# Seven block products for eight in the second MLP's first product, on one Trainium2 core

## The chip, the cores and the metric

The kernel runs on one core of one Trainium2 chip. The metric is device time of one execution in microseconds (us). The names of the engines are PE (TensorE, matrix products; PEld are its weight loads), DVE (VectorE), ACT (ScalarE), POOL (GpSimd) and SP (SyncE, which here issues every DMA).

## The reference

Attention through 32 packed queries, then two MLPs in a row over 4608 tokens of width 512. The attention output becomes `x` with shape 4608 x 512, and then:

```python
# first MLP:  w_a, w_b 512 x 1536, w_out 1536 x 512
x = ((x @ w_a) * (x @ w_b)) @ w_out
# second MLP: w_in 512 x 2048, w_out 2048 x 512
h = x @ w_in
g = h * np.clip(h + 3.0, 0.0, 6.0) / 6.0
out = g @ w_out
```

## The kernel before, in words

The program is one stream per engine, in an order written out by hand (`tc.manual_schedule`, L513): each engine takes its instructions in the order in which the Python code issues them, and waits by semaphore for what an instruction reads or overwrites. Work is set beside other work by calling small functions ("units") at chosen places of a loop.

Products in near-float32 accuracy are made of three matmuls of a rounded type (`mm3`, L57): an operand x is split into a high part, a copy in that type made by ACT, and a low part, x minus its high part, made by POOL or DVE; then hi x hi, hi x lo and lo x hi are added up in PSUM.

The first stage (L601 to L658) runs attention and the first MLP, in 4 groups of 2 batches x 12 steps (one step: 128 columns of F1). It also converts the weights of both MLPs from float64 words, piece by piece (`f64_load`, `f64_round`, `piece_units`), into float32 copies in DRAM; those of the second MLP go to `p2f`. These conversion tiles lie in the pool `main`. The pool `att` is closed at the first step of the last group (L607), and `p2a` takes its place; there the first token tile and the first weights of the second MLP are loaded and split ahead, as background units spread over the steps of that last group (L609 to L614). The first MLP's result goes to DRAM as `y1d`, transposed: 4 blocks of 128 channels x 4608 tokens.

The second MLP (L662 to L721) takes 9 tiles of 512 tokens. Per tile, for each of 16 blocks m of 128 hidden channels: `h_unit` makes h (4 channel blocks x 3 matmuls of 512 columns) into one of four PSUM banks, ACT makes `relu(h/6 + 0.5)`, DVE `min(.,1) * h`, ACT the high part and DVE the low part. Two blocks behind, `o_unit` adds the block's share to the output: 4 row blocks x 3 matmuls of 512 columns, in four PSUM banks that collect over all 16 m. All weights of the second MLP stay in SBUF, split once (`p2_weights`): three blocks ahead, the others during the first tile. The next tile's tokens are loaded and split from m = 10 on (`y_part`).

Of the kernel before, what the change touches and what calls it, by code (L numbers as in the profile page):

```python
# [8 lines left out]
F32 = mybir.dt.float32  # L9
# [13 lines left out]
P = 128  # L23
# [6 lines left out]
T2 = 512  # L30
# [14 lines left out]
def tile_kernel(ctx: ExitStack, tc: tile.TileContext, qT, kT, vn, pT, wab, wo1, win, wo2, out):  # L45
# [11 lines left out]
    def mm3(ps, l_hi, l_lo, r_hi, r_lo, first, last):  # L57
        pe.matmul(ps, lhsT=l_hi, rhs=r_hi, start=first, stop=False)  # L58
        pe.matmul(ps, lhsT=l_hi, rhs=r_lo, start=False, stop=False)  # L59
        pe.matmul(ps, lhsT=l_lo, rhs=r_hi, start=False, stop=last)  # L60
# [42 lines left out]
    y1d = dram.tile([DM // P, P, NT], F32, name="y1d")  # L103

# [247 lines left out]

    def piece_units():
# [3 lines left out]
        if m >= NM1:  # L357
            o = main.tile([P, CP], F32, tag="p2f", name=f"p2f{m}_{i}", bufs=3)
# [14 lines left out]
        u = f64_round(main, raw64.pop(k), o, f"p{m}_{i}")  # L373
# [96 lines left out]
    win_t, wo2_t = {}, {}  # L470

    def p2_weights(pool_, m, which):

        r = pool_.tile([P, CP], F32, tag="r2", name=f"r2_{m}{which}", bufs=3)
        sp.dma_start(r, p2f[m, which])

        def split():
            if which == 0:
                hi = pool_.tile([P, 4, P], F32R, tag=f"win_hi{m}", name=f"win_hi{m}")
                lo = pool_.tile([P, 4, P], F32R, tag=f"win_lo{m}", name=f"win_lo{m}")  # L480
                win_t[m] = (hi, lo)
                x = r.rearrange("p (k n) -> p k n", k=4)
            else:
                hi = pool_.tile([P, DM], F32R, tag=f"wo2_hi{m}", name=f"wo2_hi{m}")
                lo = pool_.tile([P, DM], F32R, tag=f"wo2_lo{m}", name=f"wo2_lo{m}")
                wo2_t[m] = (hi, lo)
                x = r
            act.copy(hi, x)
            pool.tensor_sub(lo, x, f32(hi))

        return split

    y_t = {}

    def y_part(pool_, tt, kk):

        r = pool_.tile([P, T2], F32, tag="r2", name=f"yr{tt}_{kk}", bufs=3)
        sp.dma_start(r, y1d[kk, :, tt * T2:(tt + 1) * T2])

        def split():  # L500
            if kk == 0:
                y_t[tt] = (
                    pool_.tile([P, 4, T2], F32R, tag="y_hi", name=f"y_hi{tt}"),
                    pool_.tile([P, 4, T2], F32R, tag="y_lo", name=f"y_lo{tt}"),
                )
# [76 lines left out]
    p2_list = [(m, w) for m in range(NM2) for w in range(2)]  # L582
    PRE = 3
# [17 lines left out]
    for t in range(NSTEP):  # L601
# [27 lines left out]
        if t == NG * NM1 - NM1:  # L629
            sp.dma_start(*stores[-1])  # L630
# [31 lines left out]
    with (  # L662
# [3 lines left out]
        gq = {}  # L666

        def h_unit(tt, m):
            ps = ps2.tile([P, T2], F32, tag="h", name=f"h{tt}_{m}", bufs=4)
            yh, yl = y_t[tt]  # L670
            wh, wl = win_t[m]
            for kk in range(4):
                mm3(ps, wh[:, kk, :], wl[:, kk, :], yh[:, kk, :], yl[:, kk, :], kk == 0, kk == 3)
            r = p2b.tile([P, T2], F32, tag="r", name=f"r{tt}_{m}", bufs=2)
            act.activation(r, ps, AF.Relu, bias=half_b, scale=1.0 / 6.0)  # L675
            u = p2b.tile([P, T2], F32, tag="u", name=f"u{tt}_{m}", bufs=2)
            dve.scalar_tensor_tensor(u, in0=r, scalar=1.0, in1=ps, op0=ALU.min, op1=ALU.mult)  # L677
            hi = p2b.tile([P, T2], F32R, tag="g2_hi", name=f"g2_hi{tt}_{m}", bufs=4)
            lo = p2b.tile([P, T2], F32R, tag="g2_lo", name=f"g2_lo{tt}_{m}", bufs=4)
            act.copy(hi, u)  # L680
            dve.tensor_sub(lo, u, f32(hi))
            gq[tt, m] = (hi, lo)
# [3 lines left out]
        def o_unit(tt, m):  # L686
            hi, lo = gq.pop((tt, m))
            wh, wl = wo2_t[m]
            for j in range(T2 // P):
                if m == 0:  # L690
                    y2[j] = ps2.tile([P, DM], F32, tag=f"o{j}", name=f"o{tt}_{j}", bufs=1)
                ts = slice(j * P, (j + 1) * P)
                mm3(y2[j], hi[:, ts], lo[:, ts], wh, wl, m == 0, m == NM2 - 1)
                if m == NM2 - 1:
                    o = p2b.tile([P, DM], F32, tag="o", name=f"os{tt}_{j}", bufs=4)
# [66 lines left out]
```

## Time and profile before

| | before |
|---|---|
| median of 3 runs | 1605.7 us (1605.18 to 1605.84) |
| profiled execution, its own time | 1605.02 us |
| its span, first to last instruction | 1603.0 us |
| PE busy / PEld | 1538.5 us (96%) / 1327.5 us (83%) |
| DVE / ACT / POOL busy | 699.2 us (44%) / 621.0 us (39%) / 406.6 us (25%) |
| mean granted TensorE clock | 0.982 |
| DMA | 149.05 MB, mean 93 GB/s |

Busy times are sums over the whole span, and the stages differ: a share says little until it is read for one stage. Matmuls are pipelined, so that the time shown for one matmul is longer than the step from its start to the start of the next; where matmuls follow each other without a break, the step is what one of them costs. The granted clock is a share of full speed.

### The profile page before, as it was taken

Reading aid. Unit: us, or ns where it says so; the run is one execution under the profiler, and the core shown is the slowest. Engines: PE = TensorE matmul, PEld = TensorE weight load, DVE = VectorE, ACT = ScalarE, POOL = GpSimd, SP = SyncE. Lnnn points to the kernel's source line nnn. Section 1 sums busy time; section 2 is a strip of 40 time slices with the busy share of each in tenths; the row PEclk is TensorE's granted clock in tenths of the full one; section 3 lists DMA queues with packets and bytes.
Section 4 is the critical chain, followed back from the end, with each engine's and each line's share of the span. In section 5 each row is a group of like instructions: output and inputs, shape, how many; then the busy total and the mean of one; then the engine's idle time right before and its main releaser. Section 6 shows DMA issues by size and latency. Waiting matters only on the chain.

```text
span 1603.0 us, 26633 instructions
## 1 busy us (share of the span) xinstructions
PE 1538.5 (96%) x10840; PEld 1327.5 (83%) x10840; DVE 699.2 (44%) x1235; ACT 621.0 (39%) x1287; POOL 406.6 (25%) x426
## 2 busy tenths in 40 slices
PE   4598999989999899999999999999999999999999
PEld 2487999888988899999988888888888888888887
DVE  5677885555754666333333233232323232322322
ACT  4465644554555444443244222232222222222322
POOL 2566554353534445334344000000000000000000
PEclk8698999999999999999999999999999999999999
DMA  8665464645365432421143101000010101010000
GB/s 279 208 213 168 156 210 155 195 165 164 127 197 180 142 112 94 138 69 53 40 131 92 47 7 47 7 27 21 7 46 8 46 7 46 7 47 7 27 1 27
DMA packets 69754, 149.05 MB, mean 93 GB/s; under 512 B 7168, under 2 KB 25600, under 8 KB 69632
## 3 DMA queue, kind: packets, MB, share of 16 engines
q1 hardware_dynamic: 69632, 147.35, 28.0%
q8 instruction: 85, 1.39, 0.4%
q14 instruction: 37, 0.30, 0.1%
HBM read 110.62 MB, written 36.70 MB: 92 GB/s over the span
## 4 chain that ended last, share of the span: by engine, by line
PE 90%; DVE 4%; ACT 3%; issue 1%; DMA 1%; POOL 0%; SPq 0%; DVEq 0%; ACTq 0%
PE h L58 8%; PE o L58 8%; PE h L60 8%; PE o L60 8%; PE h L59 8%; PE o L59 8%; PE y L58 7%; PE y L59 6%; PE y L60 6%; PE ab L58 6%; PE ab L60 6%; PE ab L59 6%; PE pw L410 2%; PE s L174 1%; DVE cv_ap L87 1%
## 5 line engine op out<-in xcount | busy, mean ns | idle before, releaser
L677 DVE SCALAR_TENSOR_TENSOR u<-r,h 128x512 f32<-128x512 f32 x144 | 99.2, 689 | 454.1 <-ACT r L675 454.0
L675 ACT ACTIVATE r<-h,half_b 128x512 f32<-128x512 f32 x144 | 99.1, 688 | 441.1 <-PE h L60 441.1
L58 PE MATMUL ab<-at_hi,pw_hi 128*128 128x288 f32 x768 | 234.5, 305 | 21.5 <-ACT a L436 18.5
L60 PE MATMUL ab<-at_hi,pw_lo 128*128 128x288 f32 x768 | 229.8, 299 | 4.0 <-DVE pw_lo L416 4.0
L58 PE MATMUL y<-g_hi,wo_hi 128*128 128x288 f32 x768 | 232.7, 303 | 0.4 <-DVE acc L465 0.4
L59 PE MATMUL ab<-at_lo,pw_hi 128*128 128x288 f32 x768 | 229.5, 299 | 1.7 <-POOL at_lo L290 1.7
L59 PE MATMUL y<-g_lo,wo_hi 128*128 128x288 f32 x768 | 228.1, 297 | 0.0
L60 PE MATMUL y<-g_hi,wo_lo 128*128 128x288 f32 x768 | 227.4, 296 | 0.0
L58 PE MATMUL h<-y_hi,win_hi 128*128 128x512 f32 x576 | 226.2, 393 | 0.0
L58 PE MATMUL o<-wo_hi,g_hi 128*128 128x512 f32 x576 | 226.0, 392 | 0.0
L60 PE MATMUL h<-y_hi,win_lo 128*128 128x512 f32 x576 | 225.4, 391 | 0.0
L60 PE MATMUL o<-wo_hi,g_lo 128*128 128x512 f32 x576 | 225.2, 391 | 0.0
L59 PE MATMUL h<-y_lo,win_hi 128*128 128x512 f32 x576 | 225.0, 391 | 0.0
L59 PE MATMUL o<-wo_lo,g_hi 128*128 128x512 f32 x576 | 224.7, 390 | 0.0
L445 POOL TENSOR_TENSOR g_lo<-g,g_hi 128x288 fp32r<-128x288 f32 x192 | 162.0, 847 | 186.3 <-ACT g_hi L444 179.0
L438 DVE TENSOR_TENSOR g<-a,ab 128x288 f32<-128x288 f32 x192 | 86.8, 452 | 205.1 <-PE ab L60 142.9
L58 PEld LDWEIGHTS ab<-at_hi,pw_hi 128*128 128x128 f32 x768 | 147.1, 192 | 34.1 <-ACT a L436 20.8
L58 PEld LDWEIGHTS y<-g_hi,wo_hi 128*128 128x128 f32 x768 | 145.6, 190 | 19.1 <-issue 7.1
L60 PEld LDWEIGHTS ab<-at_hi,pw_lo 128*128 128x128 f32 x768 | 147.1, 191 | 4.5 <-DVE pw_lo L416 4.4
L59 PEld LDWEIGHTS ab<-at_lo,pw_hi 128*128 128x128 f32 x768 | 147.3, 192 | 2.2 <-POOL at_lo L290 2.2
L59 PEld LDWEIGHTS y<-g_lo,wo_hi 128*128 128x128 f32 x768 | 145.7, 190 | 0.0
L60 PEld LDWEIGHTS y<-g_hi,wo_lo 128*128 128x128 f32 x768 | 145.6, 190 | 0.0
(80 smaller groups left out, 2194.3 us busy)
## 6 DMA issues: line engine op xcount, KB each, us to landing
rab<-wabf SPq DMA_DIRECT2D x36, 512.0 KB, 4.4
f64p<-in_wo SPq DMA_DIRECT2D x28, 512.0 KB, 3.7
f64p<-in_wab SPq DMA_DIRECT2D x24, 512.0 KB, 4.4
k<-in_kT SPq DMA_DIRECT2D x16, 576.0 KB, 5.6
q<-in_qT SPq DMA_DIRECT2D x16, 576.0 KB, 5.0
ro<-wo1f SPq DMA_DIRECT2D x36, 256.0 KB, 2.9
y1d<-acc SPq DMA_DIRECT2D x64, 144.0 KB, 1.8
yr<-y1d SPq DMA_DIRECT2D x36, 256.0 KB, 3.5
```

Of the source, the lines that this page charges most:

```text
L58: pe.matmul(ps, lhsT=l_hi, rhs=r_hi, start=first, stop=False)
L59: pe.matmul(ps, lhsT=l_hi, rhs=r_lo, start=False, stop=False)
L60: pe.matmul(ps, lhsT=l_lo, rhs=r_hi, start=False, stop=last)
L87: dve.scalar_tensor_tensor(a, in0=w, scalar=0xC0000000, in1=a, op0=ALU.bitwise_and, op1=ALU.bitwise_or)
L174: pe.matmul(ps[c][o, :SH], lhsT=lhsT[r, q, :], rhs=kq_t[n, b, q // 2][r, q % 2, ts], start=True, stop=True)
L410: pe.matmul(ps[c][o, b, :], lhsT=l[r, b, q, :], rhs=w[r, q, :], start=True, stop=True)
L438: dve.tensor_mul(g32, a, ps[1])
L445: pool.tensor_sub(gl, g32, f32(gh))
L675: act.activation(r, ps, AF.Relu, bias=half_b, scale=1.0 / 6.0)
L677: dve.scalar_tensor_tensor(u, in0=r, scalar=1.0, in1=ps, op0=ALU.min, op1=ALU.mult)
```

## The change

Only the second MLP changes, and where its operands are prepared. Tokens now come in 6 tiles of 768 (two halves of 384), hidden channels in 8 pairs p of two 128-channel blocks. With the four 256-channel x 128-channel blocks of the weights of a pair as A (A21 and A22 are the second block's) and the four 256-channel x 384-token blocks of a token tile as B, the four blocks of h come from seven products:

- S1 = A21 + A22, S2 = S1 - A11, S3 = A11 - A21, S4 = A12 - S2 (weights); T1 = B12 - B11, T2 = B22 - T1, T3 = B22 - B12, T4 = B21 - T2 (tokens)
- M1 = A11 B11, M2 = A12 B21, M3 = S4 B22, M4 = A22 T4, M5 = S1 T1, M6 = S2 T2, M7 = S3 T3
- h(0,0) = M1 + M2; with U2 = M1 + M6 and U3 = U2 + M7: h(1,1) = U3 + M5, h(1,0) = U3 + M4, h(0,1) = U2 + M5 + M3

M2, M7, M4 and M3 are added in PSUM onto M1, M6, M6 + M7 and M5; the other sums are made by DVE from a copy of M1 (`s1`, by ACT) and PSUM. The products use two PSUM banks in turn, the output six (six row blocks of 128 tokens). Each product is 2 x 3 matmuls of 384 columns; the output product keeps its 3 matmuls of 512 columns per row block and hidden block. The output units of a pair run inside the next pair's pass: `before.pop()()` does the last split of the pair before and puts its 12 output units on a list, from which `o_units(n)` takes n; `some(n)` takes n of the waiting side units (weights, tokens).

The weight operands of a pair (7 blocks, high and low, 14 KB per partition) are built by `w_prep` from `p2f`: pair 0 during the last group of the first MLP, pair p + 1 during pass p of the first token tile; the float32 words go into a tile `raw` of one buffer, which the token tiles use too. Each is stored to a DRAM tensor `w2d`, and in the five later token tiles it is loaded from there, one pass ahead, into the other of two buffers (`p2a`, `p2b`). The output weights stay in SBUF. `y_units` loads a token tile, makes T1 to T4 on POOL and splits the seven operands; in the last pass of a tile each is replaced as soon as its product is done (`swap`).

Elsewhere: the conversion tiles (`f64_load`, `f64_round`, `p2f`) lie in `att`, and the last `p2f` store is issued ahead of closing `att`, not after that step's units are set up.

```diff
-T2 = 512
+TP, TH = 768, 384
+NW = NM2 // 2
...
+    w2d = dram.tile([NW, P, 14 * 256], F32, name="w2d")
...
-            raw64[k] = f64_load(main, src, f"p{m}_{i}")
+            raw64[k] = f64_load(att, src, f"p{m}_{i}")
...
+    PROD = {1: (0, "B11"), 2: (1, "B21"), 3: (6, "B22"), 4: (2, "T4"), 5: (3, "T1"), 6: (4, "T2"), 7: (5, "T3")}
...
+    def w_load(pool_, p, tt):
+        sp.dma_start(f32(w_tile(pool_, p, tt).rearrange("p h a k n -> p (h a k n)")), w2d[p])
+
+    def w_prep(rpool, pool_, p):
...
+        def load():
+            z["r"] = rpool.tile([P, 6, CP], F32, tag="raw", name=f"raw_w{p}")
+            for i in range(2):
+                sp.dma_start(z["r"][:, i], p2f[2 * p + i, 0])
+
+        def sums(lo):
...
+                if lo:
+                    pool.tensor_sub(s3, a11, a21)
+                    pool.tensor_sub(s4, a12, s2)
+                else:
+                    pool.tensor_add(s1, a21, a22)
+                    pool.tensor_sub(s2, s1, a11)
...
+        def parts(of, a, n):
...
+                act.copy(hi, x)
+                pool.tensor_sub(lo, x, f32(hi))
...
+        def wo_load():
+            for i in range(2):
+                sp.dma_start(z["r"][:, 4 + i], p2f[2 * p + i, 1])
...
+        return [load, wo_load, sums(0), sums(1), parts(0, 0, 2), parts(3, 2, 1), parts(4, 3, 4), store], lambda o: [wo_parts(o, 0), wo_parts(o, 1)]
+
+    def y_units(pool_, tt):
...
+        def load():
+            z["r"] = pool_.tile([P, 4, TP], F32, tag="raw", name=f"raw_y{tt}")
...
         if m == 0 and g + 1 == NG:
+            sp.dma_start(*stores[-1])
             es_att.close()
...
+            y_load, y_first, y_part = y_units(p2a, 0)
+            prep, wo_prep = w_prep(p2a, p2a, 0)
+            bg = [y_load, lambda: None, lambda: None] + y_first + [y_part[k] for k in (1, 6, 2, 7, 5, 4, 3)] + prep
...
+        def prod(ps, k, first):
+            a, n = PROD[k]
+            w = w_t[now[1]]
+            yh, yl = y_t[n]
+            for c in range(2):
+                mm3(ps, w[:, 0, a, c], w[:, 1, a, c], yh[:, c], yl[:, c], first and c == 0, c == 1, not first)
...
+        side.extend(wo_prep(p2b))
         for tt in range(NTT):
+            for p in range(NW):
...
+                if tt == 0 and p + 1 < NW:
+                    prep, wo_prep = w_prep(p2a, wpool, p + 1)
+                    side.extend(prep + wo_prep(p2b))
+                elif p + 1 < NW or more:
+                    side.append(lambda x=(wpool, nxt, tt + (p + 1) // NW): w_load(*x))
+                last = p == NW - 1 and more
+                if more and p == NW - 2:
+                    y_load, y_first, y_part = y_units(p2a, tt + 1)
+                    side.extend([y_load, lambda: None, lambda: None] + y_first)
...
+                x = bank2("x")
+                prod(x, 1, True)
+                s1 = tmp("s1", 2)
+                act.copy(s1, x)
+                if before:
+                    before.pop()()
+                swap(1)
+                o_units(2)
+                some(3)
+                y = bank2("y")
+                prod(y, 6, True)
+                u2 = plus("u2", 2, s1, y)
+                swap(6)
+                prod(x, 2, False)
+                gate(0, 0, x)
+                swap(2)
+                o_units(2)
+                some(2)
+                prod(y, 7, False)
+                u3 = plus("u3", 2, s1, y)
+                parts(0, 0)
+                swap(7)
+                x = bank2("z")
+                prod(x, 5, True)
+                c22 = plus("c22", 2, u3, x)
+                gate(1, 1, c22)
+                swap(5)
+                o_units(2)
+                some(2)
+                prod(y, 4, False)
+                c21 = plus("c21", 1, s1, y)
+                parts(1, 1)
+                gate(1, 0, c21)
+                swap(4)
+                prod(x, 3, False)
+                c12 = plus("c12", 2, u2, x)
+                parts(1, 0)
+                gate(0, 1, c12)
+                swap(3)
+                o_units(2)
+                some(2)
+                o_units(4)
+                some(9)
```

## Rows read from the trace of the kernel before

**Rows 1.** The page, parts 1 and 4: busy time by engine; the last chain.
```profile
PE 1538.5 (96%) x10840; PEld 1327.5 (83%) x10840; DVE 699.2 (44%) x1235; ACT 621.0 (39%) x1287; POOL 406.6 (25%) x426
...
PE 90%; DVE 4%; ACT 3%; issue 1%; DMA 1%; POOL 0%; SPq 0%; DVEq 0%; ACTq 0%
```

**Rows 2.** Busy by stretch: PE, PEld, DVE, ACT, POOL; clock, DMA share, GB/s.
```profile
600.00:800.00 200.00, 199.62 (x1802) 190.32 (x1801) 81.61 (x166) 82.12 (x200) 82.01 (x98) 1.00 0.24 78
...
1100.00:1200.00 100.00, 100.00 (x440) 82.38 (x440) 28.49 (x42) 26.63 (x42) 0.00 (x0) 1.00 0.07 22
```

**Rows 3.** Waits: total us, times, longest.
```profile
ACT r L675 <- PE h L60: 441.1, 140, 3.7
```

**Rows 4.** Timeline where the second MLP begins: start, duration, engine, operation [idle before].
```profile
799.85 0.29 PE L60 MATMUL y<-g_hi,wo_lo 128*128 128x288 f32 x1
...
807.45 0.29 PE L60 MATMUL y<-g_hi,wo_lo 128*128 128x288 f32 x1
807.58 0.40 PE L58 MATMUL h<-y_hi,win_hi 128*128 128x512 f32 x1
...
807.78 0.46 DVE L465 TENSOR_TENSOR acc<-y,acc 128x288 f32<-128x288 f32 x1 [0.74 <-PE y L60]
```

**Rows 5.** Timeline, the last matmul.
```profile
1599.01 0.39 PE L60 MATMUL o<-wo_hi,g_lo 128*128 128x512 f32 x1
```

**Rows 6.** Groups of instructions by form: busy us, mean ns, idle before.
```profile
L681 DVE TENSOR_TENSOR g_lo<-u,g_hi 128x512 fp32r<-128x512 f32 x144 | 99.8, 693 | 98.9 <-ACT g_hi L680 98.9
...
L465 DVE TENSOR_TENSOR acc<-y,acc 128x288 f32<-128x288 f32 x192 | 86.8, 453 | 95.8 <-PE y L60 95.1
...
L394 POOL TENSOR_TENSOR wo_lo<-ro,wo_hi 128x256 fp32r<-128x256 f32 x96 | 75.0, 781 | 139.4 <-ACT wo_hi L393 136.1 <-PE y L60 3.3
...
L393 ACT CAST wo_hi<-ro 128x256 fp32r<-128x256 f32 x96 | 39.6, 413 | 34.4 <-PE y L59 26.5 <-POOL ro L95 7.9
...
L489 POOL TENSOR_TENSOR wo_lo<-r,wo_hi 128x512 fp32r<-128x512 f32 x16 | 20.7, 1295 | 28.1 <-ACT wo_hi L488 16.2 <-PE o L60 11.9
...
L488 ACT CAST win_hi<-r 128x512 fp32r<-128x512 f32 x16 | 9.9, 618 | 22.8 <-DMA r<-p2f 22.8
```

**Rows 7.** DMA issues: KB each, median us from issue to landing.
```profile
rab<-wabf SPq DMA_DIRECT2D x36, 512.0 KB, 4.4
...
r<-p2f SPq DMA_DIRECT2D x32, 256.0 KB, 2.8
```

**Rows 8.** Timeline of SP at the end of the first token tile.
```profile
902.35 1.80 SPq L700 DMA_DIRECT2D out<-os  x4
904.19 1.80 SPq L498 DMA_DIRECT2D yr<-y1d  x3
```

**Rows 9.** Busy by stretch of 1 us, the first and last of six (last two columns: DMA).
```profile
903.00:904.00 1.00, 1.00 (x6) 0.77 (x5) 0.00 (x0) 0.00 (x0) 0.00 (x0) 1.00 0.82 305
...
908.00:909.00 1.00, 1.00 (x6) 0.84 (x5) 0.00 (x0) 0.00 (x0) 0.00 (x0) 1.00 0.59 225
```

**Rows 10.** Timelines of DVE and of POOL, 862 to 875 us.
```profile
863.91 0.75 DVE L508 TENSOR_TENSOR y_lo<-yr,y_hi 128x512 fp32r<-128x512 f32 x1 [0.97 <-ACT y_hi L507]
...
870.56 1.37 DVE L508 TENSOR_TENSOR y_lo<-yr,y_hi 128x512 fp32r<-128x512 f32 x1 [2.08 <-ACT y_hi L507]
...
864.07 1.75 POOL L489 TENSOR_TENSOR win_lo<-r,win_hi 128x512 fp32r<-128x512 f32 x1
...
870.09 1.30 POOL L489 TENSOR_TENSOR win_lo<-r,win_hi 128x512 fp32r<-128x512 f32 x1 [0.44 <-ACT win_hi L488]
```

**Rows 11.** Timeline of PE and busy by stretch, behind a gap in the first stage.
```profile
80.16 0.90 PE L202 MATMUL et<-ident,ex 128*128 128x128 f32 x3 [6.58 <-ACT ex L197]
...
76.00:80.00 4.00, 0.00 (x0) 0.00 (x0) 3.83 (x7) 1.17 (x3) 3.01 (x3) 0.50 0.97 337
80.00:84.00 4.00, 3.84 (x20) 3.69 (x20) 3.86 (x7) 4.00 (x12) 2.55 (x3) 0.63 0.77 277
84.00:88.00 4.00, 3.12 (x23) 2.63 (x21) 3.86 (x5) 1.11 (x3) 2.81 (x3) 1.00 0.67 217
```

More of the change, by code (lines that the diff above doesn't have):

```diff
@@ new lines, in y_units, with blk, get, add @@
+    def y_units(pool_, tt):
+        z = {}
+        def load():
+            z["r"] = pool_.tile([P, 4, TP], F32, tag="raw", name=f"raw_y{tt}")
+            for k in range(4):
+                sp.dma_start(z["r"][:, k], y1d[k, :, tt * TP:(tt + 1) * TP])
+        def blk(n):
+            k, j = int(n[1]) - 1, int(n[2]) - 1
+            return z["r"][:, 2 * k:2 * k + 2, j * TH:(j + 1) * TH]
+        def get(n):
+            return blk(n) if n[0] == "B" else z[n]
+        def add(to, a, b):
+            def fn():
+                z[to] = pool_.tile([P, 2, TH], F32, tag="ty", name=f"ty{tt}_{to}", bufs=3)
+                pool.tensor_sub(z[to], get(a), get(b))
+            return fn
+        def part(n):
+            def fn():
+                hi = pool_.tile([P, 2, TH], F32R, tag=f"yh{n}", name=f"yh{tt}_{n}")
+                lo = pool_.tile([P, 2, TH], F32R, tag=f"yl{n}", name=f"yl{tt}_{n}")
+                y_t[n] = (hi, lo)
+                act.copy(hi, get(n))
+                (pool if n[0] == "B" else dve).tensor_sub(lo, get(n), f32(hi))
+            return fn
+        first = [add("T1", "B12", "B11"), add("T2", "B22", "T1"), add("T3", "B22", "B12")]
+        t4 = add("T4", "B21", "T2")
+        def part4():
+            t4()
+            part("T4")()
+        return load, first, {1: part("B11"), 6: part("T2"), 2: part("B21"), 7: part("T3"), 5: part("T1"), 4: part4, 3: part("B22")}
@@ L680, in h_unit, with parts, o_unit @@
+        def parts(i, j):
+            n = 1 if i == j else 2
+            hi, lo = tmp(f"g2h{i}{j}", n, F32R), tmp(f"g2l{i}{j}", n, F32R)
+            u = u_t.pop((i, j))
             act.copy(hi, u)
             dve.tensor_sub(lo, u, f32(hi))
-            gq[tt, m] = (hi, lo)
+            g_t2[i, j] = (hi, lo)
         y2 = {}
-        def o_unit(tt, m):
-            hi, lo = gq.pop((tt, m))
+        def o_unit(tt, p, i, j, k, hi, lo):
+            n, m = 3 * j + k, 2 * p + i
             wh, wl = wo2_t[m]
[L689 to L695, printed above, removed]
-                    if j % 2:
-                        act.copy(o, y2[j])
-                    else:
-                        dve.tensor_copy(o, y2[j])
-                    sp.dma_start(out[tt * T2 + j * P:tt * T2 + (j + 1) * P, :], o)
@@ L720, in tile_kernel @@
-        for x in prev:
-            o_unit(*x)
+            first, last = p == 0 and i == j, p == NW - 1 and i != j
+            if first:
+                y2[n] = ps2.tile([P, DM], F32, tag=f"o{n}", name=f"o{tt}_{n}", bufs=1)
+            ts = slice(k * P, (k + 1) * P)
+            mm3(y2[n], hi[:, ts], lo[:, ts], wh, wl, first, last)
+            if last:
+                o = p2b.tile([P, DM], F32, tag="o", name=f"os{tt}_{n}", bufs=3)
+                if n % 2:
+                    act.copy(o, y2[n])
+                else:
+                    dve.tensor_copy(o, y2[n])
+                sp.dma_start(out[tt * TP + n * P:tt * TP + (n + 1) * P, :], o)
```

147 lines of the change are left out of this document (73 added, 74 removed).

## The prediction

> **What bounds the kernel now.** I read the busy shares first: TensorE (PE) is busy 96% of the span, and the chain of work that ended last lies 90% on PE [rows 1]. Next the table by stretches: from 600 us on PE is busy in practically every microsecond at a granted clock of 1.00, and in the second MLP VectorE (DVE) and ScalarE (ACT) fill less than a third of a 100 us stretch and GpSimd (POOL) nothing [rows 2]. The waits say it from the other side: ACT's gate stood 441.1 us in all behind PE [rows 3]. So the second MLP is as long as its matmuls, and a change there is worth its matmul time, less every microsecond for which something else newly holds PE up.
>
> The profiled execution took 1605.02 us: the span of 1603.0 us and 2.0 us around it. The median of the runs is 1605.7 us, 0.04% above; I add to 1605.0. A measurement of this kernel can tell about 0.2% (3.2 us) from no change.
>
> **Part 1: the matmuls.** Before, 9 tiles x 16 blocks x 4 x 3 = 1728 matmuls of 512 columns make h, and as many make the output. The stage runs from the first h matmul at 807.58 to the last o matmul at 1599.01 plus one step, without a break: 791.7 us / 3456 = 0.2291 us each [rows 4, 5]. After, the first product takes 6 tiles x 8 pairs x 7 products x 2 x 3 = 2016 matmuls of 384 columns; the second product keeps its 1728. No row has 384 columns. The nearest are 512 (0.2291) and 288: from 799.85 to 807.45 stand 57 steps of y matmuls, 0.1333 us each [rows 4]. The line between them gives 0.1743 at 384. From below, the 512 row in proportion to columns gives 0.1718; from above, the weight load, one per matmul, would set the pace if it had to be done alone (rival 3). I take 0.1743: the 288-column matmuls, each with its own weight load, run faster than that. So 1728 x 0.2291 = 395.8 us becomes 2016 x 0.1743 = 351.4 us: **-44.4 us** (-49.5 by proportion).
>
> **Part 2: a steady pass.** One pass (tile, pair) is 7 products of 6 x 0.1743 = 1.05 us and 12 output units of 3 x 0.2291 = 0.69 us: 15.57 us of PE. Beside it stand 13 DVE operations of 384 columns, 0.55 us each (between 0.453 at 288 and 0.693 at 512), 7.2 us; and 9 of ACT at 0.52, 4.7 us [rows 6]. Two PSUM banks take turns: M6's bank needs u2 read before M7, M5 needs the bank that gate(0,0) reads, M4 needs u3, M3 needs c22. A read starts 0.33 us after the last matmul of a product started [rows 4]. In PE order the tightest of these is M5: M2 ends 4.5 us into the pass, the gate (ACT 0.55, DVE 0.55) is through at 6.1, M5's turn is 6.95. Cost zero; without the output units in between (the first pass) it is 0.7 us. From the second tile on each pass reads 1.83 MB of finished weights, issued as soon as M3 of the pass before frees the tile and due 19 us later. 512 KB land in 4.4 us, 256 KB in 2.8 [rows 7]: 12.4 us by that slope. Hidden.
>
> **Part 3: the first tile, where the weights are built.** Here a chain runs beside PE, and it goes through one "raw" tile (one buffer) and through POOL. Per pair: load two blocks; 4 sums on POOL of 256 columns; the low parts of 2, 1 and 4 blocks on POOL; then a 1.83 MB store; then two low parts of the output weight, which free "raw" for the next load. POOL needs 0.78 us at 256 columns and 1.30 at 512 [rows 6], so 2.4 at 1024: 4 x 0.78 + 1.30 + 0.78 + 2.4 = 7.6, with handovers 7.8 us from landing (call it L) to the last part, and 2.6 more until "raw" is free.
> - *Second pass.* Pair 1's load must wait for pair 0's output weights, which are split only after M1 of the first pass: ACT 1.25 to 2.9, POOL to 4.9 us, then 3.5 us for the load (2.8, a second issue 0.45 later and the handover [rows 7, 8]): L = 8.4 us after the stage begins. PE has nothing but the seven products then and ends at 8.0. M1 waits for L + 4.5, M6 for L + 7.8 = 16.2 instead of 9.75.
> - *Each further pass.* The store goes to SyncE's queue at L + 7.9, the next load behind it at L + 10.4. What is the rate? Four stores and three loads, 1.84 MB, issued from 902.35 on, moved from about 903 to 908.6 [rows 8, 9]: some 330 GB/s. So 5.5 us for the store, 1.6 for the 0.5 MB behind it, 0.6 to begin and 0.6 to report: the next L is at L + 16.1. If the load didn't stand behind the store, L + 13.6, and PE's 15.57 would rule; by the slope of rows 7 the two take 14 us and L is at L + 22. I take 16.1, since rows 9 show the engines with as much queued.
> - *A port.* POOL's low part at 864.07 took 1.75 us where others took 1.30, and a DVE subtraction at 870.56 took 1.37 where 0.69 is usual: each overlapped a subtraction of the other engine [rows 10]. A pass has 4 such DVE subtractions of 0.55. At worst all lie in POOL's way, 2.2 us; with POOL's part of the chain half the pass and either engine losing as often, 0.5. The cycle is 16.6 us against PE's 15.57.
> - The Trainium skill ("SBUF — State Buffer", section "Who interferes with whom") says that a VectorE instruction with two SBUF inputs and a GpSimd instruction that reads SBUF exclude each other for a whole instruction; by that rule the worst case would be four full blocks a pass, 6 x 1.7 = 10 us on my sum; the two lengthened rows agree with the rule, while most subtractions before missed each other.
> - *ACT's order.* ACT copies the blocks of the next pair (it waits for L) ahead of its part of g(0,0), whose DVE half stands ahead of c22, which M3 waits for. So M3 comes no earlier than L + 2.4, and M6 of the next pass, 7.6 us of PE work later, at L + 10. PE's seven passes: M6 of the eighth is at 8.4 + 6 x 16.6 + 10 = 118.0, against 7.3 + 6 x 15.57 + 2.4 = 103.1 undisturbed. **+14.9 us.**
>
> **Part 4: first tile to second.** The next tile's tokens go through "raw" too. In tile 0 their load (1.57 MB) can be issued only at L + 10.4 of the last pair, behind its store; the halves land at L + 16.8 and 19.1. POOL forms T1 and T2 (1.84 us each at 768 columns) by 21.0, and ACT, in order, copies B11 and T2 before it reaches gate(0,0): copy 21.9, DVE's part of T2 22.9, gate 23.5. M5 starts at L + 23.6; its undisturbed turn is L + 10 + 4.5. **+9.1 us.** In the later tiles "raw" has long been free, the load goes out one pass before it is needed (3.4 MB at 330 GB/s, 10.3 us, with POOL's sums 16 of 17 us): 0 to 1 us each at four borders; I take 0.3.
>
> **Part 5: small things.** After a PE gap of 6.58 us ending at 80.16 the granted clock was at 0.50, the lower of its two levels (1.2 and 2.4 GHz), then 0.63 on average over four microseconds, and 1.00 behind them [rows 11]: some 1.5 us lost per gap of that kind. Two are made here (4.9 and 9.1 us): **+3.0** (0 to 5). The conversion tiles move to another pool and the last p2f store moves ahead of closing it: on SyncE's queue only the next output-weight load stands behind that store, due a step of 16 us later; zero, at most the 2.8 us that 256 KB take [rows 7]. Tile 0's operands are built during the last quarter of the first MLP: two pieces per step, POOL 82 of 200 us busy there [rows 2]; 0 to 2, I take 0.4. The end: the last g takes 3.3 us while PE still has ten output units; the copy and store after it stay. Zero.
>
> Sum: -44.4 + 14.9 + 9.1 + 3.0 + 1.2 + 0.4 = -15.8: **1589 us**.
>
> **Rivals.**
> 1. *The building is hidden.* If loads don't wait behind the store, PE's own pass rules: only the second pass's 6.4 us, a shorter border (6) and one clock drop stay, 14 us: 1575, down to 1568 if the border goes too. For it: SyncE issues early, and 16 engines share the work. Against: one "raw" buffer. Chance 0.18.
> 2. *The chain on "raw" rules the first tile outright.* One mechanism: load, POOL, store, each waiting for the one before, at the slower transfer rate of rows 7 (L to L 22 us). Then 6 x 5.4 = 32 us more than my sum: 1621, slower. It breaks even from a cycle of 19.2 us (6 x 2.6 = 15.8). For it: single transfers are the rows of rows 7, and the port adds to the same chain. Against: rows 9. Chance 0.22, over the stretch 1597 to 1625.
> 3. *Weight loads set the pace* at 384 columns. The loads are shown at 187 ns (82.4 us busy for 440 loads [rows 2]); at that pace 2016 take 377 us, the gain falls to 18: 1615. Against: y matmuls with the same loads run at 133 ns. Chance 0.03.
> 4. *Later weights land late.* 40 loads, due in 19 us; it decides only from 19 us a load. Chance 0.02.
> That the change does less arithmetic is certain from its loops; only its cover is open.
>
> **Chances.** The forecast (stalls of 20 to 36 us, 1581 to 1597) 0.55; rival 1 0.18; rival 2 0.22, of which 0.05 below 1602.5, 0.07 within 0.2%, 0.10 above; rivals 3 and 4 0.05, nearly all above, 0.01 within. Faster 0.78, same 0.08, slower 0.14. The range 1574 to 1606 leaves out 0.07 below and 0.13 above.
>
> **What would show it.** Steps of 0.174 us between matmuls of 384 columns; a PE gap of about 5 us some 8 us after the second MLP begins, ended by POOL's low part; passes of 16 to 17 us in the first tile (about 148 us in all) and of 15.6 in the others (124.6 a tile); a gap of about 9 us in the first tile's last pass, ended by DVE's gate, with the tokens' load landing late; granted clock below 1 only behind these gaps. I am wrong if PE stands in the later tiles, if the step is nearer 0.19 us, or if the store doesn't hold back the load behind it.

## The result, and the profile after

The changed kernel takes **1588.64 us** (median of 4 runs, 1588.37 to 1590.18) against 1605.44 us for the kernel before beside it (1603.48 to 1605.84): a ratio of 0.990, 95% interval 0.9883 to 0.9917. The profiled execution took 1588.73 us with a span of 1587.0. Forecast: 1589, so faster, and by the size that was worked out: 1% less, clear of noise. The sum came out; some of its terms did not, and the experiments are about those.

The page of the kernel after, parts 1 and 4 (compare [rows 1]):
```profile
PE 1499.7 (95%) x11128; PEld 1353.8 (85%) x11128; DVE 874.9 (55%) x1559; ACT 682.0 (43%) x1445; POOL 528.8 (33%) x508
...
PE 77%; DVE 5%; POOL 5%; issue 4%; ACT 4%; DMA 4%; SPq 1%; DVEq 0%; POOLq 0%; ACTq 0%
```
PE has 38.8 us less busy time, but the span fell by only 16.0, and the last chain now runs 77% on PE where it ran 90%. The other 22.8 us are new idle time of PE.

Where? First a later tile, then the first. The timeline of PE inside a later tile (start, duration, engine, operation, [idle before]), and the windows 1100 to 1200 (columns as in [rows 2]):
```profile
1107.11 0.33 PE L59 MATMUL h_2x<-yh_B,w 128*128 128x384 f32 x1
...
1107.98 0.34 PE L61 MATMUL h_2x<-yh_B,w 128*128 128x384 f32 x1
...
970.52 0.45 PE L59 MATMUL h_1x<-yh_B,w 128*128 128x384 f32 x1 [0.21 <-ACT s L822]
...
1581.42 0.39 PE L61 MATMUL o<-wo_hi,g2l 128*128 128x512 f32 x1
```
```profile
1100.00:1200.00 100.00, 100.00 (x503) 90.42 (x502) 50.40 (x88) 35.92 (x64) 11.37 (x6) 1.00 0.39 142
```
Five steps in 0.87 us are 0.174 us each at 384 columns, as interpolated, and PE has no idle time in the window. Passes there take 15.50 us. The only stall in these tiles is one per tile, as at 970.52: that pass takes 15.98, because the copy M2 waits for stands on ACT behind an output copy, and ACT's output copies wait for stores (six outputs go through a staging tile of three buffers).

Now the first tile. The start of M6 (`h_py`) marks a pass. From the first pass on it starts at 807.23, 822.99, 841.10, 857.89, 874.96, 891.62, 908.01 and 924.67, and in the next tile at 953.60. So the second starts 15.76 us after the first, six passes of 16.39 to 18.11 follow, and the border takes 28.93. The timeline of PE with the waits longest in this stretch, and one of each repeated kind:
```profile
819.50 0.69 PE L61 MATMUL h_1x<-yh_B,w 128*128 128x384 f32 x1 [4.41 <-POOL w L518]
...
832.21 0.44 PE L59 MATMUL h_1z<-yh_B,w 128*128 128x384 f32 x1 [1.11 <-DVE c L744]
...
841.10 0.41 PE L59 MATMUL h_2y<-yh_T,w 128*128 128x384 f32 x1 [1.07 <-ACT g2h L759]
...
893.25 0.44 PE L59 MATMUL h_5x<-yh_B,w 128*128 128x384 f32 x1 [0.43 <-ACT s L822]
...
926.57 0.44 PE L59 MATMUL h_7x<-yh_B,w 128*128 128x384 f32 x1 [0.69 <-ACT s L822]
...
940.20 0.69 PE L59 MATMUL h_7z<-yh_T,w 128*128 128x384 f32 x1 [9.71 <-DVE u L753]
```
The two large gaps are the two that were forecast, with the releasers that were forecast (POOL's low part; DVE's gate). Between them stand small waits: six at M2 for ACT's copy `s`, one at M6 for ACT's high part `g2h`, and only two at M3 for `c22`, where the forecast had put them all.

The windows around the border show what the gap does to the granted clock:
```profile
935.00:940.00 5.00, 0.00 (x0) 0.00 (x0) 2.00 (x2) 2.03 (x3) 4.70 (x3) 0.50 0.66 278
940.00:945.00 5.00, 4.80 (x13) 4.22 (x14) 4.57 (x5) 1.41 (x3) 4.11 (x3) 0.50 0.00 0
945.00:950.00 5.00, 5.00 (x26) 4.52 (x25) 4.08 (x6) 3.45 (x6) 1.20 (x1) 0.98 0.36 89
```
13 matmuls start in the 5 us behind the gap, 26 in the next 5.

One pass of the first tile, read across the engines (timelines of POOL, DVE, ACT and SP, 882 to 899 us). This is the reading on which the experiments rest:
```profile
882.02 0.73 POOL L507 TENSOR_TENSOR raw_w<-raw_w 128x256 f32<-128x256 f32 x1 [3.52 <-DMA raw_w<-p2f]
...
885.50 4.70 POOL L518 TENSOR_TENSOR w<-raw_w,w 128x512 fp32r<-128x512 f32 x3
892.38 2.54 POOL L534 TENSOR_TENSOR wo_lo<-raw_w,wo_hi 128x512 fp32r<-128x512 f32 x2 [2.18 <-ACT wo_hi L533]
898.37 0.74 POOL L507 TENSOR_TENSOR raw_w<-raw_w 128x256 f32<-128x256 f32 x1 [3.44 <-DMA raw_w<-p2f]
...
887.83 2.78 DVE L753 SCALAR_TENSOR_TENSOR u<-r,c 128x384 f32<-128x384 f32 x1
...
890.65 0.51 ACT L759 CAST g2h<-u 128x384 fp32r<-128x384 f32 x1 [3.10 <-DVE u L753]
...
891.70 1.12 ACT L533 CAST wo_hi<-raw_w 128x512 fp32r<-128x512 f32 x2
892.73 0.47 ACT L822 COPY s<-h_5x 128x384 f32<-128x384 f32 x1
...
890.23 0.32 SPq L522 DMA_DIRECT2D w2d<-w  x1
894.95 0.80 SPq L496 DMA_DIRECT2D raw_w<-p2f  x2
```
L, the landing, is at 882.02, the next at 898.37: 16.35 us, where 16.1 was forecast. But the way there is another. DVE's gate takes 2.78 us instead of 0.55, held until POOL's long low part ends; ACT stands 3.10 us behind it and, in order, reaches the copies of the output weight only at 891.70; POOL splits them from 892.38 and frees `raw` at L + 12.9, not L + 10.4. The load then goes out 4.7 us behind the store, which itself lands in 5.7 (the median of the eight), and so takes 3.4 us instead of 5.7. Both errors were 2.3 to 2.5 us, with opposite signs. ACT's copy `s` for M2 is behind the same two copies: hence the waits at M2. The chain that ended last, in order of time, runs through this ring and not through PE from 808.5 to 940 us; the pass above in it:
```profile
886.75 3.44 POOL w L518 x2
890.20 2.14 issue
892.38 2.55 POOL wo_lo L534 x2
895.31 2.92 DMA raw_w<-p2f
```

### The profile page after: what moved, and what is told of

It is laid out like the page before. It is cut to its first block, busy times and chain, and to the rows that moved or that the text cites. A ratio compares the mean times of both kernels' runs of the same rounds, so it can differ in the third digit from the quotient of the medians.

```text
span 1587.0 us, 27985 instructions
## 1 busy us (share of the span) xinstructions
PE 1499.7 (95%) x11128; PEld 1353.8 (85%) x11128; DVE 874.9 (55%) x1559; ACT 682.0 (43%) x1445; POOL 528.8 (33%) x508
## 4 chain that ended last, share of the span: by engine, by line
PE 77%; DVE 5%; POOL 5%; issue 4%; ACT 4%; DMA 4%; SPq 1%; DVEq 0%; POOLq 0%; ACTq 0%
PE o L60 7%; PE o L61 7%; PE o L59 7%; PE y L59 6%; PE y L60 6%; PE y L61 6%; PE ab L59 6%; PE ab L61 6%; PE ab L60 6%; PE pw L412 2%; POOL w L518 2%; DMA raw_w<-p2f 2%; POOL wo_lo L534 1%; PE s L176 1%; DMA out<-os 1%
## 5 line engine op out<-in xcount | busy, mean ns | idle before, releaser
L60 PE MATMUL o<-wo_lo,g2h 128*128 128x512 f32 x576 | 225.7, 392 | 0.0
L61 PE MATMUL o<-wo_hi,g2l 128*128 128x512 f32 x576 | 225.6, 392 | 0.0
L59 PE MATMUL o<-wo_hi,g2h 128*128 128x512 f32 x576 | 225.4, 391 | 0.0
L760 DVE TENSOR_TENSOR g2l<-u,g2h 128x384 fp32r<-128x384 f32 x192 | 129.9, 677 | 149.0 <-ACT g2h L759 143.9
L558 POOL TENSOR_TENSOR ty_T<-raw_y 128x768 f32<-128x768 f32 x12 | 23.3, 1945 | 385.6 <-DMA raw_y<-y1d 385.6
L751 ACT ACTIVATE r<-c,half_b 128x384 f32<-128x384 f32 x144 | 88.9, 617 | 136.7 <-DVE c L744 136.2
L759 ACT CAST g2h<-u 128x384 fp32r<-128x384 f32 x192 | 98.7, 514 | 98.3 <-DVE u L753 96.9
L438 ACT COPY a<-ab 128x288 f32<-128x288 f32 x192 | 76.2, 401 | 148.6 <-PE ab L61 147.0
```

The lines of the kernel that those rows point to most:

```text
L59: pe.matmul(ps, lhsT=l_hi, rhs=r_hi, start=first, stop=False, skip_group_check=skip)
L60: pe.matmul(ps, lhsT=l_hi, rhs=r_lo, start=False, stop=False, skip_group_check=skip)
L61: pe.matmul(ps, lhsT=l_lo, rhs=r_hi, start=False, stop=last, skip_group_check=skip)
L438: act.copy(a, ps[0])
L558: pool.tensor_sub(z[to], get(a), get(b))
L751: act.activation(r, c, AF.Relu, bias=half_b, scale=1.0 / 6.0)
```

## The experiments

Three theories for the passes of the first tile. **A**, the forecast's: the load lands late since it stands behind the 1.83 MB store. **B**: ACT's order frees `raw` late. **C**: DVE's gate waits for POOL's long subtraction at a shared port. All times are medians of four runs or more, ratios are to the kernel before in the same job, and "first tile" is the time from its first M6 to the second tile's. Without any stall that would be 117.2 us: 8.7 to the second M6 (six products and one more, two output units) and 7 x 15.50. The medians of the kernel before lie between 1604.0 and 1605.4 us in these jobs, so that 1 or 2 us between two of the kernels are hardly more than that spread; the traces tell such differences better.

| | us | ratio (95% interval) | first tile, us |
|---|---|---|---|
| after | 1588.64 | 0.990 (0.9883 to 0.9917) | 146.4 |
| e1_store_behind | 1586.55 | 0.989 (0.9875 to 0.9905) | 142.8 |
| e2_split_low | 1595.12 | 0.9945 (0.993 to 0.996) | 152.4 |
| e3_out_early | 1584.38 | 0.9874 (0.9858 to 0.9891) | 142.6 |
| e4_no_build | 1566.39 | 0.9761 (0.9747 to 0.9776) | 123.1 |
| e5_both_orders | 1579.35 | 0.9843 (0.9829 to 0.9858) | 136.0 |
| e8_second_pass | 1587.79 | 0.9895 (0.9878 to 0.9911) | 145.8 |
| e6_all_ahead | 1607.57 | 1.0023 (1.0014 to 1.0032) | 164.3 |
| e9_second_pass_b | 1584.35 | 0.9877 (0.986 to 0.9893) | 139.4 |
| e10_all_ahead_b | 1577.71 | 0.9836 (0.9821 to 0.9851) | 134.2 |
| e11_both_and_second | 1574.69 | 0.981 (0.9797 to 0.9824) | 131.2 |

**e1_store_behind** puts the store behind the next pair's loads.
```diff
+                    held.append(prep[-1])
+                    prep[-1] = lambda: None
+                    if p > 0:
+                        prep[1] = lambda a=prep[1], b=held.pop(0): (a(), b())
...
```


> In the first token tile each pair's store to w2d is issued behind the next pair's two loads (and the last pair's behind the next tile's token load) instead of ahead of them; nothing else moves. Theory A (as predicted): the load stands some 2.5 us behind the store in the queue and this sets the first tile's cycle; then passes go from 16.4-17.1 to PE's 15.5 us, the token load lands 5 us sooner, the gap of 9.7 us falls to about 5, and the time to 1574-1577. Theory B (ACT's order frees the raw tile late, and the trace of after shows a load landing 4.4 us behind its issue where one alone took 3.3): only about 1.1 us a pass and at the border are won, 1580-1583. Theory C (the DVE gate that waits 2.2 us for POOL's long low part sets the pass): nothing in the passes, at most 1-2 us at the border, 1587.

Passes of 15.51 to 16.68, border 28.97: 2 us faster, where A expected over 11, B 5 to 9 and C 1 or 2. With no store ahead of it POOL has the load 3.4 to 3.8 us after its issue, no sooner than the 3.4 of the pass shown above. A as the ruling link of these passes is refuted; PE still waits at M2 for ACT.

What e1 wins lies mostly in the second pass. There the change's load does stand close behind the store, and M3 waits for what comes of it (832.21 in the timeline of PE above). Timelines of SP and POOL, the change, then e1:
```profile
822.85 0.32 SPq L522 DMA_DIRECT2D w2d<-w  x1
825.69 1.60 SPq L496 DMA_DIRECT2D raw_w<-p2f  x2
...
832.21 0.73 POOL L507 TENSOR_TENSOR raw_w<-raw_w 128x256 f32<-128x256 f32 x1 [6.54 <-DMA raw_w<-p2f]
...
826.69 0.79 SPq L496 DMA_DIRECT2D raw_w<-p2f  x2
...
830.26 0.74 POOL L507 TENSOR_TENSOR raw_w<-raw_w 128x256 f32<-128x256 f32 x1 [3.60 <-DMA raw_w<-p2f]
```
6.5 us from issue to POOL, 2.8 us behind the store, became 3.6, and the next M6 follows after 16.32 us instead of 18.11.

**e2_split_low** cuts POOL's long subtraction into pieces of 256 columns, so that DVE waits for one piece only.
```diff
-                pool.tensor_sub(lo, x, f32(hi))
+                for i in range(0, n * 256, 256):
+                    pool.tensor_sub(lo[:, i:i + 256], x[:, i:i + 256], f32(hi[:, i:i + 256]))
```


> POOL's low part of 1024 columns is made by four subtractions of 256 columns, and the one of 512 by two, so that POOL works about 0.9 us longer per pair but no single subtraction lasts over 0.75 us. Theory C: the DVE gate on h(1,0), 2.75 us in the first tile where 0.56 is usual, falls to about 1.3, ACT's next copy of M1 comes 1.4 us sooner, passes go to 15.5-15.8 us, and the time to 1581-1584. Theory A: POOL's longer stretch makes the chain through the raw tile 0.9 us longer per pass, 1589-1594. Theory B: in between, 1586-1590, since ACT frees the raw tile sooner but POOL ends later.

Timelines of POOL, DVE and SP, the same pass:
```profile
889.10 5.92 POOL L519 TENSOR_TENSOR w<-raw_w,w 128x256 fp32r<-128x256 f32 x7
...
891.59 1.10 DVE L754 SCALAR_TENSOR_TENSOR u<-r,c 128x384 f32<-128x384 f32 x1
...
895.05 0.32 SPq L523 DMA_DIRECT2D w2d<-w  x1
898.22 1.46 SPq L496 DMA_DIRECT2D raw_w<-p2f  x2
```
DVE's hold fell from 2.78 to 1.10, as C said. But POOL's low parts took 5.92 us instead of 4.70, and the store left only 3.2 us ahead of the load, which POOL then had 4.4 to 5.8 us after its issue. Passes grew to between 15.5 and 20.6, with waits of 1.2 to 2.6 us at M3 for `c22`: the forecast's own stall. So A's link is real and decides as soon as C's is shortened; the time is 1 us above A's range and far from C's.

**e3_out_early** takes three more side units behind M5, so that the output weight is split in the slot of its pair's low parts.
```diff
-                some(2)
+                some(5 if tt == 0 and p > 0 else 2)
```


> In passes 1 to 6 of the first tile the two output weight blocks are split right behind the last low part of the pair (ahead of g(1,1) and the gates of h(1,0) and h(0,1) in ACT's order), not behind M3. Theory B: the raw tile is free 2.2 us sooner per pass, the passes fall to PE's 15.5 us and the token load lands 2 us sooner: 1578-1581. Theory A: the load then stands the longer behind the store and lands no more than 0.5 us sooner: 1585-1588. Theory C: POOL holds the port still longer while the gate waits, passes 1 to 2 us longer: 1592-1600.

4.3 us faster than the change: passes 15.74 to 17.60, border 26.79. B's link is worth some, not all, and the trace shows where the rest went. Timelines of SP and POOL, one pass:
```profile
888.47 0.32 SPq L522 DMA_DIRECT2D w2d<-w  x1
891.63 1.48 SPq L496 DMA_DIRECT2D raw_w<-p2f  x2
...
896.50 1.11 POOL L507 TENSOR_TENSOR raw_w<-raw_w 128x256 f32<-128x256 f32 x1 [4.90 <-DMA raw_w<-p2f]
```
`raw` is free at L + 11.2 (L is 880.44 here) instead of L + 12.9, but its load now stands 3.2 us behind the store instead of 4.7, and takes 4.9 us instead of 3.4: A's link took back some 1.5 of the 1.7 us. The waits of PE are now at M6, for ACT's `g2h` (five, 0.2 to 0.9 us).

**e4_no_build** leaves the building of pairs 1 to 7 out of the first tile; every pass loads and uses pair 0's operands, while the split of the output weights stays.
```diff
-        sp.dma_start(f32(w_tile(pool_, p, tt).rearrange("p h a k n -> p (h a k n)")), w2d[p])
+        sp.dma_start(f32(w_tile(pool_, p, tt).rearrange("p h a k n -> p (h a k n)")), w2d[0])
...
-                    side.extend(prep + wo_prep(p2b))
+                    side.append(lambda x=(wpool, nxt, tt): w_load(*x))
+                    side.extend([lambda: None, prep[1], lambda: None] + wo_prep(p2b))
```


> Left out: the operands of pairs 1 to 7 are not built; every pass loads pair 0's operands from w2d in their place, so the output is wrong by that. The matmuls, gates and output weights stay. All theories: the first tile's passes take 15.5 us like the others, the gap of 4.4 us at its second pass and the 9.7 us at its border go, and with them the clock at 0.50 behind the border: 28 to 29 us less than the changed kernel, 1559-1562. If it stays above 1570, the first tile is held up by something other than the building.

From the third pass on they take 15.49 to 15.51, the border 17.95; 22.3 us are gone. So 23.2 of the 29.2 us that the first tile loses are the building's. The time is 4 us above the expectation: the other 6 stay with this kernel's own second pass (gaps of 0.68 for the loaded operands and 1.27 for DVE) and border.

**e5_both_orders** is e1 and e3 together.

> Both orders at once: the store behind the next loads (as in e1_store_behind) and the output weights split early (as in e3_out_early). Alone they won 2 and 4 us. If the first tile's cycle is one loop through the raw tile (load, POOL, ACT's order, raw free), with the store as one link of it, both links shortened leave it under PE's 15.5 us: passes 3 to 7 at 15.5 to 15.6, the token load in the border lands 4 to 5 us sooner, gap about 5, 1575-1578. If the port (DVE's gate behind POOL's long subtraction) sets the pass by itself, passes stay at 16 and more and the time at 1582-1584.

Passes of 16.26, 16.38 and then 15.49 to 15.50: from the third M6 on PE's own pace, as expected of one loop. 2.1 us and 4.3 us alone, 9.3 together (in the first tile 3.6, 3.8 and 10.4). That is the sign of one closed loop: load, POOL's sums and low parts, DVE's gate held at the port, ACT's stream, `raw` free, load. A single link shortened moves the wait to the next; the loop no longer decides once its whole length is below PE's 15.5. C by itself does not set the pass: DVE is still held here (2.53 us for a subtraction at 850.24, 1.66 for the gate behind it), and in these passes PE waits for nothing. The time is 1.4 us above the expected range; the border stays, with a gap of 7.92 where 5 was expected, ended by DVE's gate as in the change (timeline of PE):
```profile
930.57 0.69 PE L59 MATMUL h_7z<-yh_T,w 128*128 128x384 f32 x1 [7.92 <-DVE u L753]
```

**e8_second_pass** loads pair 1 and forms its sums during the first MLP, and gives pair 0's output weights a place of their own.
```diff
+            prep1, wo_prep1 = w_prep(p2a, lambda: p2b, 1)
+            wo_load0 = prep.pop(1)
...
+            bg += [prep1[0], prep1[2], prep1[3]]
...
-        side.extend(wo_prep(p2b))
+        _, wl1, _, _, pa, pb, pc, st = prep1
+        side.extend([lambda: wo_load0(p2b), pa, pc] + wo_prep(p2b) + [pb, st, wl1, lambda: None] + wo_prep1(p2b))
```


> Only the start of the stage changes: pair 0's output weights go through tiles of the output staging buffer, so that pair 1's load and its four sums on POOL are done during the first MLP; pair 1's low parts come first in the first pass. Prediction as made: the second pass waits for pair 1 through the raw tile; then the gap of 4.4 us and the late M6 of the second pass go: M6 of pass 1 stands 9.7-10.5 us behind the stage's first matmul plus 1.05 (16.8 before), and the raw tile is free 7 us sooner for pair 2: 8 us less by the second pass, of which the cycle of the later passes keeps nothing back: 1579-1582. Rival: the gap only moves to the third pass, because pair 2's load is what is late: 1586-1588.

The second M6 comes 11.28 us after the first (15.76 in the change), the third 22.94 after that. Timelines of ACT, SP and PE:
```profile
825.58 1.26 ACT L534 CAST wo_hi<-raw_w 128x512 fp32r<-128x512 f32 x2 [5.01 <-DMA raw_w<-p2f]
...
818.25 0.32 SPq L522 DMA_DIRECT2D w2d<-w  x1
818.62 1.39 SPq L527 DMA_DIRECT2D raw_w<-p2f  x2
...
827.27 0.69 PE L59 MATMUL h_1x<-yh_B,w 128*128 128x384 f32 x1 [5.32 <-ACT s L829]
```
The output weight's load is queued 0.4 us behind the store and lands about 7 us after its issue; ACT stands 5.01 us at the copy that needs it, with the copy for M2 behind. This is A's mechanism in its plainest form: a small load right behind the 1.83 MB store. The time is that of the rival (1586 to 1588), but not by its reason: what was late was this load, not pair 2's.

**e9_second_pass_b** moves that load into the first MLP too.
```diff
-            bg += [prep1[0], prep1[2], prep1[3]]
+            bg += [prep1[0], prep1[1], prep1[2], prep1[3]]
```


> As e8_second_pass, but pair 1's two output blocks are loaded in the first MLP as well, so that no copy of ACT in the first pass waits for a load that stands behind the 1.83 MB store. In e8_second_pass ACT waited 5.0 us for that load, its copy of M1 stood behind, and M2 of the second pass came 5.3 us late. If that wait was all that ate the gain: gap of the second pass under 1 us, M6 of the third pass 6 to 8 us sooner than in the changed kernel relative to the stage's start, 1580-1583. If pair 2's own chain is what is late: the loss only moves to the third pass again, 1586-1588.

Second M6 after 11.26, the third 16.06 later; first tile 7.0 us shorter, time 4.3 less, 1.4 us above the expected range. The gap of the second pass is 1.56 us, where less than 1 was expected. The stage began 2.5 us later in the profile of this kernel than in that of the change (808.70 against 806.19).

**e6_all_ahead** loads every pair one pass earlier, with the output weight's load behind the store.
```diff
+                    def both(a=ld, b=st):
+                        a()
+                        b()
...
+                        side.extend([pa, pc, pb, both, wl_o, nop, nop, wo[0], sm[0], wo[1]] + sm[1:])
```


> All output weights of the first tile go through the output staging tiles, so that the raw tile is free behind a pair's last low part; the next pair's load (in the last passes the next tile's tokens) goes out there, ahead of the store, and its sums run on POOL a pass ahead of their use. If the whole loss of the change in its first tile is the chain through the raw tile, no PE gap over 1 us stays in the first tile: passes of 15.5, border 15.5 to 17, clock at 1.00 throughout: 1588.6 less 28.8 us, 1559-1563. If the port holds up DVE whatever the order, passes stay at 16 to 16.5: 1563-1568. If tokens still land late at the border: 1566-1570.

A miss of some 40 us, slower than the kernel before. Passes of 20.2 to 21.1, behind one of 25.65; PE stands 2.9 to 3.4 us a pass at M5 for DVE's gate. ACT once more, each pass:
```profile
883.62 1.28 ACT L534 CAST wo_hi<-ro 128x512 fp32r<-128x512 f32 x2 [3.29 <-DMA ro<-p2f]
```
ACT waits for the output weight's load, which is queued behind the store, and the copy for M2 and the splits that POOL waits for stand behind it. A pass is some 5 us longer than 15.5; how much of that is this wait, only the next kernels tell.

**e10_all_ahead_b** is e6 with those loads, and the splits that need them, in another order: the load goes out some 16 us ahead of its split.
```diff
+                    wo_next = (lambda f=wl: f(p2b), wo)
...
+                        side.extend([wo_now[0], nop, nop, pa, nop, pc, both] + wo_now[1] + sm)
```


> As e6_all_ahead, with the order mended: a pair's output blocks are loaded at the start of the pass behind the one that builds its operands, ahead of any store of that pass, and POOL makes the next pair's sums with nothing of ACT's in front of them. In e6_all_ahead ACT stood 3 us per pass at copies of output blocks whose load lay behind the store, and POOL's sums stood behind those. If the chain through the raw tile and ACT's order are the whole loss: passes of 15.5 us, gap at the second pass under 1 us, at the border 2 to 4 us: 1562-1567. If POOL's port holds DVE up in any order: passes 16 to 16.5, 1567-1572.

29.9 us faster than e6 by that order alone, 10.9 faster than the change, but 6 us above even the slower of the two expectations. Passes of 16.20 to 16.41, which is what the expectation had put to the port; PE stands at one place in each. Timelines of DVE and PE:
```profile
828.68 2.14 DVE L764 TENSOR_TENSOR g2l<-u,g2h 128x384 fp32r<-128x384 f32 x1 [0.23 <-ACT g2h L763]
...
834.92 0.50 PE L60 MATMUL o<-wo_lo,g2h 128*128 128x512 f32 x1 [0.66 <-POOL wo_lo L535]
```
An output product waits for POOL's low part, a split that this order does just ahead of its use. The port stands on the way to it: ACT waits 2.69 us for the gate behind the held subtraction (until 831.86), then copies the output weight, and POOL splits it. How the missing time divides between that order, the port and the border (25.38) was not tried.

**e11_both_and_second** is e5 with e9's second pass.

> Pair 1's loads and sums in the first MLP (the edit of e9_second_pass_b) together with both shortened links of the loop: the store behind the next pair's loads, and the output weight's two splits of a pair in the same slot as its low parts (the edits of e5_both_orders). If the second pass and the loop of the later passes are two separate losses, their gains add: seventh M6 as early against the start of the stage as in e5_both_orders less the second pass's 5 us, passes of 15.5 from the third or fourth on, border as in e5_both_orders (25.8): 1573 to 1576. Rival: the second pass's stall had served the loop as slack, so that passes 2 to 6 now take 16 to 17 us until the chain has caught up with PE, and the total stays within 1.5 us of e5_both_orders: 1578 to 1581. Second rival: the loop's load of the third pair is queued behind a 1.83 MB store in the second pass and PE stands there: 1580 or more.

1574.69 us (1572.96 to 1574.96): in the total the gains add (9.3 and 4.3 make 13.6, measured 14.0), as expected of two separate losses. In the first tile alone they do not quite: 10.4 and 7.0 became 15.1, since both edits shorten the way to the third M6. It is the fastest version here. M6 intervals 11.26, 16.88, 15.59, then 15.49 to 15.50, border 25.52. Timeline of PE, the two largest waits left in the tile:
```profile
817.06 0.41 PE L59 MATMUL h_1x<-yh_B,w 128*128 128x384 f32 x1 [1.57 <-ACT g2h L763]
...
925.78 0.69 PE L59 MATMUL h_7z<-yh_T,w 128*128 128x384 f32 x1 [7.12 <-DVE u L757]
```
Of the 14 us that its first tile still loses, 10 are the border: the second tile's tokens, loaded through `raw` last.

## Why the prediction was right

| step | forecast, us | measured, us |
|---|---|---|
| matmuls | -44.4 | -47.7 |
| eighth pass's M6 late, second pass included | +14.9 | +15.7 |
| border gap | +9.1 | +9.7, and 0.7 at M2 |
| clock behind the gaps | +3.0 | +2.4 at the border, and 0.6 beside the listed waits; 1.4 more lie in the 15.7 |
| later tiles, small things | +1.6 | +2.3 |
| end and start | 0 | +1.6 and -1.4 |
| sum | -15.8 | -16.1 |

The measured column goes by the two profiled executions, whose spans differ by 16.0 us; the medians differ by 16.8.

*Matmuls:* the 48 passes at 15.50 us are 744.0 against the 791.7 of before [rows 4, 5]. The step by interpolation was right to 0.001 us; the 0.07 us by which a pass is shorter than 15.57 make 3.4 over the stage. Rival 3 falls: loads stay hidden at 0.174 us a step.

*Second pass:* a gap of 4.41 us, which begins 8.9 us into the stage (806.19) and is ended by POOL: some 5 us, some 8 us in, were forecast. L was 8.3 us into the stage, forecast 8.4. M6 was 7.1 late (822.99 against 815.9), not 6.4. Of the 7.1 only 4.6 are the stop at that gap; 1.4 are the clock (from 819.50 to 822.99 the steps take 3.49 us instead of 2.06), and 1.1 are two short stops for DVE, at M5 (810.74) and at the next pass's M1 (814.49). So the wait for POOL was put some 2 us too long, and two costs that the term did not hold hid it. One of them Part 2 had priced: 0.7 at M5 in a pass without output units, which the 9.75 leaves out.

*Further passes:* from landing to landing it took 16.8 us on average (16.0 to 17.7), 16.6 were forecast: right by two errors that cancel. (Rival 1, with PE's 15.57 in these passes, and rival 2, with 22, both fall.) The rule that the store holds back the load held wherever the load came close behind it: in the change's second pass, in e2, e3, e6 and e8 the load was there 7.3 to 9.5 us after the store's issue, though it went out 0.4 to 3.2 us behind; the forecast's prices make 8.3. What failed is the distance. It was put at 2.5 us, because `raw` was taken to be free at L + 10.4; in five of six passes it was 4.7, and there the load took 3.4 to 4.5 us, little more than the 3.4 to 3.8 that it takes with no store ahead (e1). So e1 gained 2 us where the forecast's distance would give 11. What had made `raw` late was the loop shown above, and the term mis-sized was the **port**: 0.5 us a pass was taken, while the gate alone lost 2.2 on the chain. The worst case of 2.2 in the forecast was another thing, four DVE subtractions in POOL's way; that one of POOL's long subtractions stops DVE was not priced, and ACT behind DVE, and POOL's last split behind ACT (its wait of 2.18 us at 892.38), were not followed.

The groups of DVE in the first tile (806.2 to 948) and in a later one (1072 to 1197) show the port apart from the rest (busy us, mean ns, idle before):
```profile
L760 DVE TENSOR_TENSOR g2l<-u,g2h 128x384 fp32r<-128x384 f32 x30 | 28.7, 956 | 31.8 <-ACT g2h L759 30.9
L753 DVE SCALAR_TENSOR_TENSOR u<-r,c 128x384 f32<-128x384 f32 x22 | 27.7, 1259 | 6.3 <-ACT r L751 5.9
...
L744 DVE TENSOR_TENSOR u<-s,h_5y 128x384 f32<-128x384 f32 x2 | 1.1, 548 | 0.9 <-PE h_5y L61 0.9
...
L760 DVE TENSOR_TENSOR g2l<-u,g2h 128x384 fp32r<-128x384 f32 x32 | 20.6, 643 | 22.9 <-ACT g2h L759 22.1
L753 DVE SCALAR_TENSOR_TENSOR u<-r,c 128x384 f32<-128x384 f32 x24 | 14.3, 598 | 8.6 <-ACT r L751 8.1
```
In the first tile, where POOL is at work most of the time, the two forms that read two SBUF tiles take 956 and 1259 ns on average, in the later tile 643 and 598; the form that reads one of its two inputs from PSUM takes 548 in the first tile too. The forecast counted four such operations a pass, the subtractions; the three gates that read `c` from SBUF belonged on the list, and it was a gate that stood on the chain.

The rule of the Trainium skill ("SBUF — State Buffer", section "Who interferes with whom"), weighed in the forecast and then discounted, agrees with these rows: an instruction waits out the other engine's whole instruction (2.78 us instead of 0.55 at 887.83), and those with a PSUM input are untouched.

*Border:* a gap of 9.71 at 940.20, by the forecast's route: the tokens' load is issued late, POOL forms T1 and T2, ACT and DVE split T2, then the gate. The clock behind it cost 2.4 us where 1.5 was forecast: 28.93 less 15.50, 9.71 and 0.69 leaves 3.0, of which 2.2 lie between 940.20 and 944.84, where 12 matmuls take 4.64 us instead of 2.41, and 0.2 in the two steps behind them. The rest is what a wait costs beyond its listed idle time.

*Later tiles:* 1792 KB loads land in 7.3 us; rival 4 falls. The forecast had the borders at 0.3 each; they cost nothing, and one pass a tile costs 0.48 for the output staging. The start of the stage (806.19, before 807.58) is no term of the change: over the kernels here it lies between 806.2 and 808.7, and three with the same work ahead of it (e8, e6, e10) differ by 2 us. The end is 1.6 us longer, with six outputs through three staging buffers instead of four, which was costed at zero. Most of the rise of the DMA volume (149 to 237 MB) is the 40 loads of finished weights, and PE waits for none of them.

What stays open: how much of the last 14 us of e11 can be had. A second `raw` tile, which would take the border's load off the loop, was not tried.

## What to carry to other kernels

Price a change of arithmetic by its steady stage, where steps interpolate to a hundredth, and then look for the place where its new operands are first made: here 6 tiles gained 48 us and the first one gave back 29. Where a load, several engines and a single buffer form a ring, work out the time around the whole ring and compare it with the engine it must keep up with; shortening one link moves the wait, and two edits worth 2 and 4 us alone are worth 9 together. On an in-order engine, ask of every instruction that waits for a transfer what stands behind it.

## What the runs showed of the hardware

- A VectorE operation with two SBUF inputs lost up to 2.2 us to one 1024-column GpSimd subtraction, and cutting the latter into four did shorten the operation from 2.78 to 1.10 us (e2), but made GpSimd's stretch 5.92 us instead of 4.70.
- 512 KB of loads took 3.4 to 3.8 us to their reader with no large store ahead in the queue (e1). Close behind a store of 1792 KB what counted was the store: its issue lay 7.3 to 9.5 us back when the load was there, whether the load had gone out 0.4 us behind it (e8, e6) or 3.2 (e2, e3).
- After the 9.7 us gap the clock was at the lower of its two levels (0.50, 1.2 GHz) in the window 940 to 945, in which PE worked 4.80 us, and at 0.98 in the next 5 us; after the 4.4 us gap the windows of 5 us show 0.89 and 0.76, then 1.00.
- One transfer of 1792 KB lands in 7.3 us as a load (x40) and 5.7 us as a store (x8), where the slope of [rows 7] gave 12.4:
```profile
w<-w2d SPq DMA_DIRECT2D x40, 1792.0 KB, 7.3
...
w2d<-w SPq DMA_DIRECT2D x8, 1792.0 KB, 5.7
```
